# Two MLPs behind a linear attention: the second MLP's two layers mixed product by product, with its accumulators in six PSUM banks

## The chip, the cores and the metric

The kernel runs on one core of a Trainium2 chip. TensorE (PE in the tables) multiplies; each product needs its stationary operand loaded first (PEld). ScalarE (ACT) and VectorE (DVE) do the elementwise work, GpSimd (POOL) a little, and SyncE (SP) issues the DMAs. Each engine runs its own instructions in the order in which they were written. The metric is the time of one execution on the device, in microseconds (us).

## The reference

```
attn: per batch b of 4, head h of 8, over t in 0..767, with a 48x48 state:
    y_t = r_t (state + (u*k_t) outer v_t);  state = w_t * state + k_t outer v_t
x = attn as [3072 tokens, 384]
h = x @ w_in;  g = h if h > 0 else exp(h) - 1;  x = g @ w_out        # first MLP, 384 -> 2048 -> 384
h = x @ w_in2; g = h * sigmoid(h);              out = g @ w_out2     # second MLP, same sizes
```

Everything is float32. The kernel keeps that precision by writing each operand of a product as a rounded high half and a remainder, the low half, and adding three products: high by high, high by low, low by high.

## The kernel before

The program has three stretches. At first the attention of the first four units runs alone (to about 42 us); then the first MLP runs over six blocks of 512 tokens, with the attention of the next block placed between its products (to about 540 us); then the second MLP runs over the same six blocks (to the end).

The hidden width of 2048 is cut into 16 slices (`f`). One call of `slot(m, j, ..., f)` is one slice of block `j` of MLP `m`; I call it a slot. In a slot of the second MLP:

- `hidden` issues nine first-layer products, 512 columns wide, into the accumulator `ph` (line 443). There are two `ph` banks (pool `ps_h`).
- `split_g` makes the halves `gh` (ScalarE, line 465) and `gl` (VectorE, line 466) of the slice before.
- `act_begin` applies Silu to `ph` (ScalarE, line 454).
- `flush_out` takes the slice of two slots earlier (`LAG = 2`) off the list `pend` and issues its twelve second-layer products, 384 columns wide, with 128-column pieces of `gh` and `gl` as the stationary operand (`out_second`, line 482). They add to four accumulators `po`, one for each 128 tokens. After the last slice of a block, `evac_second` copies the four accumulators out, two on ScalarE and two on VectorE, in turn (`os`, lines 507 and 509), and stores them.

So the second-layer products of a block's last slice (15) are issued in the slot of slice 1 of the next block, and the slot after it is the first with the next block's second-layer products. In the first MLP a slot is alike, but the second layer has nine products 512 wide (`out_first`, line 474), and the end of a block copies three accumulators out (`x2s`, lines 491 and 493).

The second MLP's weights are prepared below the slots of the first MLP's last block and the first slots of the second MLP: `w_join` (VectorE, lines 414 and 416), `w_scale` (ScalarE, 405 and 407), `w_split` (`wh` on ScalarE, line 428, then `wl` on VectorE, line 429), one weight slice per slot.

The order on each engine is the order of the calls (`manual_schedule`); waits are added where a tile is read or a buffer reused. PSUM has eight banks: two in `ps_h`, three each in `ps_o` and `ps_a`. The second MLP's four `po` take three of `ps_o` and one of `ps_a`.

Of the kernel before, what the change touches and what calls it, by code (L numbers as in the profile page):

```python
# [7 lines left out]
F32 = mybir.dt.float32  # L8
# [10 lines left out]
LAG = 2  # L19
# [15 lines left out]
def kernel(  # L35
# [21 lines left out]
    nc = tc.nc  # L57
    B, H, S, D = r.shape
    NT, DM = out.shape
# [6 lines left out]
    KT = DM // 128  # L66
    NF = DFF // 128
# [7 lines left out]
    ps_o = ctx.enter_context(tc.tile_pool(name="ps_o", bufs=3, space=PSUM))  # L75
    ps_a = ctx.enter_context(tc.tile_pool(name="ps_a", bufs=3, space=PSUM))
# [311 lines left out]
    wh, wl = {}, {}  # L388
# [45 lines left out]
            w_load()  # L434


    def hidden(m, xt, nt, f):
        ph = ps_h.tile([128, nt], F32, tag="h", name="ph")
        n = 0
        for kt in range(KT):  # L440
            a, b = wh["i", f][:, kt * 128:(kt + 1) * 128], wl["i", f][:, kt * 128:(kt + 1) * 128]
            for lhs, rhs in ((a, "h"), (a, "l"), (b, "h")):
                nc.tensor.matmul(ph, lhs, xt[rhs][:, kt, 0:nt], start=n == 0, stop=n == 3 * KT - 1)  # L443
                n += 1
        return ph

    def act_begin(m, ph, nt):
        g = g_p.tile([128, nt], F32, tag="g", name="g")
        if m == 0:
            nc.scalar.activation(out=g, in_=ph, func=ACTF.Exp)  # L450

            nc.scalar.activation(out=g, in_=g, func=ACTF.Relu, scale=-1.0, bias=1.0)  # L452
        else:
            nc.scalar.activation(out=g, in_=ph, func=ACTF.Silu)  # L454
        return g

    def act_end(m, g, ph):
        if m == 0:
            nc.vector.scalar_tensor_tensor(  # L459
                out=g, in0=g, scalar=-1.0, in1=ph, op0=ALU.mult, op1=ALU.max)  # L460

    def split_g(m, g, nt):
        gh = g_p.tile([128, nt], F32R, tag="gh", name="gh")
        gl = g_p.tile([128, nt], F32R, tag="gl", name="gl")
        nc.scalar.activation(out=gh, in_=g, func=ACTF.Copy)  # L465
        nc.vector.tensor_tensor(out=gl, in0=g, in1=gh.bitcast(F32), op=ALU.subtract)  # L466
        return gh, gl

    def out_first(po, gs, nt, f):
        gh, gl = gs  # L470
        for ot in range(KT):
            a, b = (t["o", f][:, ot * 128:(ot + 1) * 128] for t in (wh, wl))
            for i, (lhs, rhs) in enumerate(((a, gh), (a, gl), (b, gh))):
                nc.tensor.matmul(  # L474
                    po[ot][:, 0:nt], lhs, rhs, start=f == 0 and i == 0, stop=f == NF - 1 and i == 2)

    def out_second(po, gs, nt, f):
        gh, gl = gs
        for t in range(nt // 128):
            sl = slice(t * 128, (t + 1) * 128)  # L480
            for i, (lhs, rhs) in enumerate(((gh, wh), (gh, wl), (gl, wh))):
                nc.tensor.matmul(  # L482
                    po[t][:, 0:DM], lhs[:, sl], rhs["o", f], start=f == 0 and i == 0,
                    stop=f == NF - 1 and i == 2)

    def evac_first(po, nt, tok):
        for ot in range(KT):
            pool = stage["x"] if ot == 1 and "x" in stage else o_p
            o = pool.tile([128, nt], F32, tag="o", name="x2s")
            if ot == 1:  # L490
                nc.vector.tensor_copy(o, po[ot][:, 0:nt])
            else:
                nc.scalar.activation(out=o, in_=po[ot][:, 0:nt], func=ACTF.Copy)  # L493
            nc.sync.dma_start(x2_d[:, ot, bass.ds(tok, nt)], o)
# [5 lines left out]
    def evac_second(po, nt, tok, rows=unit_rows, pool=None, final=False):  # L500
        for t in range(nt // 128):
            o = (pool or o_p).tile([128, DM], F32, tag="o", name="os")
            cut = 0 if t % 2 else DM
            if final and t == nt // 128 - 1:
                cut = DM // 2
            if cut:
                nc.scalar.activation(out=o[:, 0:cut], in_=po[t][:, 0:cut], func=ACTF.Copy)
            if cut < DM:
                nc.vector.tensor_copy(o[:, cut:], po[t][:, cut:DM])
            nc.sync.dma_start(out[bass.ds(rows(tok + t * L), L), :], o)  # L510
# [180 lines left out]
    pend, po = [], {}  # L691
    last = None

    def flush_out():
        m, j, f, nt, tok, g = pend.pop(0)
        if f == 0:
            if m == 0:
                po[m, j] = [ps_o.tile([128, nt], F32, tag="o", name="po") for _ in range(KT)]
            else:
                po[m, j] = [ps_o.tile([128, DM], F32, tag="o", name="po") for _ in range(3)]  # L700
                po[m, j].append(ps_a.tile([128, DM], F32, tag="att", name="po"))
        (out_first, out_second)[m](po[m, j], g["s"], nt, f)
        if f == NF - 1 and m == 0:
            evac_first(po[m, j], nt, tok)
        elif f == NF - 1:
            evac_second(po[m, j], nt, tok, pool=stage["o"], final=j == NB - 1)

    def slot(m, j, xt, nt, tok, f, tick=lambda part: None):
        nonlocal last
        ph = hidden(m, xt, nt, f)  # L710
        if last is not None:
            last[1]["s"] = split_g(last[0], last[1]["g"], last[2])
        g = act_begin(m, ph, nt)
        tick(0)
        act_end(m, g, ph)
        rec = {"g": g}
        last = (m, rec, nt)
        if len(pend) >= LAG:
            flush_out()
        pend.append((m, j, f, nt, tok, rec))  # L720
        tick(1)
# [10 lines left out]
    with tc.manual_schedule():  # L732
# [25 lines left out]
        for j, units in enumerate(BLOCKS):  # L758
            nt, final = units * L, j == len(BLOCKS) - 1
# [4 lines left out]
            def tick(part):  # L764
                nonlocal at
                at += 1
                done = count - 6 * len(ticks) - len(todo)
                if alone:
                    prep_rest(at, FIRST[j + 1], alone)
                wait, end = DELAY if alone else 0, END if j == 0 else 2 * NF - 2  # L770
                while done < count and done * (end - wait) < (at - wait) * count:
                    if not todo:
                        todo.extend(round_ticks(ticks.pop(0)))
                    todo.pop(0)()
                    done += 1
                if j == 0 or final and f % 4 != 3:
                    w_tick(part)

            for f in range(NF):
                slot(0, j, xts[j], nt, FIRST[j] * L, f, tick)  # L780
                if final:
                    if f == 0:
                        attn.close()
                        far_decays(0)
                        stage_open(4)
                        stage["x"] = staging.enter_context(tc.tile_pool(name="o3", bufs=1))
                        stage["o"] = staging.enter_context(tc.tile_pool(name="o2", bufs=4))
                    if f in (2, 4):
                        far_decays(f // 2)
                    if f == 0:  # L790
                        w_start(1)
                    if f == 8:
                        load_x2(0)
                    if f in (11, 12, 13):
                        split_x2(0, f - 11)
# [5 lines left out]
        for j in range(NB):  # L801
            for f in range(NF):
                if f == 8 and j + 1 < NB:
                    load_x2(j + 1)
                if f in (11, 12, 13) and j + 1 < NB:
                    split_x2(j + 1, f - 11)
                slot(1, j, x2t[j], TB, j * TB, f, w_tick)
        last[1]["s"] = split_g(last[0], last[1]["g"], last[2])
        while pend:
            flush_out()  # L810
# [65 lines left out]
    def whole_mlp(m, nt, load, evac):  # L876
        xt = x_tile(nt)
        load(xt["l"].bitcast(F32))
        split_x(xt, slice(0, nt), xt["l"].bitcast(F32), nc.vector)
        if m == 0:  # L880
            po = [ps_o.tile([128, nt], F32, tag="o", name="po") for _ in range(KT)]
        else:
            po = [ps_o.tile([128, DM], F32, tag="o", name="po") for _ in range(3)]
            po.append(ps_a.tile([128, DM], F32, tag="att", name="po"))
        for f in range(NF):
            ph = hidden(m, xt, nt, f)
            g = act_begin(m, ph, nt)
            act_end(m, g, ph)
            (out_first, out_second)[m](po, split_g(m, g, nt), nt, f)
        evac(po)  # L890
# [101 lines left out]
```

## Time and profile before

| | |
|---|---|
| median of 3 runs | 949.76 us (948.05 to 950.05) |
| profiled execution, its own time | 947.38 us |
| its span, first to last instruction | 945.6 us |
| PE busy | 918.1 us, 97% |
| ACT, DVE busy | 502.4 us (53%), 489.4 us (52%) |
| granted TensorE clock over the span | 0.981 |

The profile is of one execution; the time beside its span holds what lies around the instructions. A busy share says how much of the span an engine had an instruction running; which engine sets the end is read from the chain of work that ended last and from who waits for whom.

### The profile page before, as it was taken

How to read it: one execution, taken by the hardware profiler on the slowest of the kernel's cores; microseconds unless marked ns; L12 is line 12 of the kernel's file. 1: busy time of each engine (PE TensorE's matmuls, PEld its weight loads, DVE VectorE, ACT ScalarE, POOL GpSimd, SP SyncE). 2: the span in 40 equal slices, each digit the busy share in tenths (PEclk: the TensorE clock that was granted, in tenths of full speed). 3: DMA queues.
4: the chain of work that ended last, by engine and by line, in shares of the span. 5: the costliest groups of instructions: out<-in, count | busy, mean ns of one | idle time of the engine just before them, and what ended most of it. 6: DMA issues, size and time to landing. Idle time of an engine off the chain costs nothing.

```text
span 945.6 us, 15205 instructions
## 1 busy us (share of the span) xinstructions
PE 918.1 (97%) x6158; PEld 790.8 (84%) x6158; DVE 489.4 (52%) x726; ACT 502.4 (53%) x901; POOL 133.9 (14%) x101
## 2 busy tenths in 40 slices
PE   7779899999999999999999999999999999999996
PEld 7667688888888888888888899999999999999996
DVE  7798877776666776666378762212212212222211
ACT  6788866665655655555488963323323333333332
POOL 0000012443453334453000000000000000000000
PEclk8799999999999999999999999999999999999998
DMA  8644414222322221220245330100200200200001
GB/s 252 184 153 161 163 48 124 69 67 57 110 67 73 91 66 57 78 68 1 101 141 193 136 99 1 67 0 1 68 1 1 68 1 1 67 1 1 34 1 37
DMA packets 32222, 68.69 MB, mean 73 GB/s; under 512 B 3600, under 2 KB 13968, under 8 KB 32144
## 3 DMA queue, kind: packets, MB, share of 16 engines
q1 hardware_dynamic: 32144, 67.64, 22.5%
q8 instruction: 50, 0.82, 0.4%
q14 instruction: 28, 0.23, 0.1%
HBM read 58.19 MB, written 9.44 MB: 72 GB/s over the span
## 4 chain that ended last, share of the span: by engine, by line
PE 89%; DVE 6%; DMA 2%; ACT 2%; issue 1%; SPq 0%; DVEq 0%; ACTq 0%
PE ph L443 40%; PE po L482 21%; PE po L474 19%; PE sc L295 2%; PE y L361 2%; PE y L342 1%; DVE wst L414 1%; PE ktp L253 1%; DVE wl L429 1%; DVE wst L416 1%; DMA in_v<-in_v_tok_dram 1%; DVE am L304 1%; DVE gl L466 1%; PE upd L316 1%; DMA above_sb<-in_above_dram 1%
## 5 line engine op out<-in xcount | busy, mean ns | idle before, releaser
L466 DVE TENSOR_TENSOR gl<-g,gh 128x512 fp32r<-128x512 f32 x192 | 144.8, 754 | 313.5 <-ACT gh L465 313.3
L443 PE MATMUL ph<-xh,wh 128*128 128x512 f32 x576 | 227.6, 395 | 2.1 <-DVE g L459 2.1
L443 PE MATMUL ph<-xh,wl 128*128 128x512 f32 x576 | 227.4, 395 | 0.0
L443 PE MATMUL ph<-xl,wh 128*128 128x512 f32 x576 | 227.2, 394 | 0.0
L465 ACT ACTIVATE gh<-g 128x512 fp32r<-128x512 f32 x192 | 120.8, 629 | 153.7 <-PE po L482 109.7
L454 ACT ACTIVATE g<-ph 128x512 f32<-128x512 f32 x96 | 57.4, 598 | 137.8 <-PE ph L443 137.1
L482 PE MATMUL po<-wh,gl 128*128 128x384 f32 x384 | 129.5, 337 | 0.0
L482 PE MATMUL po<-wh,gh 128*128 128x384 f32 x384 | 129.3, 337 | 0.0
L482 PE MATMUL po<-wl,gh 128*128 128x384 f32 x384 | 128.9, 336 | 0.0
L443 PEld LDWEIGHTS ph<-xh,wl 128*128 128x128 f32 x576 | 108.7, 189 | 23.5
L443 PEld LDWEIGHTS ph<-xh,wh 128*128 128x128 f32 x576 | 109.1, 189 | 22.4 <-DVE g L459 2.5
L443 PEld LDWEIGHTS ph<-xl,wh 128*128 128x128 f32 x576 | 108.8, 189 | 19.5
L474 PE MATMUL po<-gh,wh 128*128 128x512 f32 x288 | 114.7, 398 | 0.0
L474 PE MATMUL po<-gl,wh 128*128 128x512 f32 x288 | 113.0, 392 | 0.0
L474 PE MATMUL po<-gh,wl 128*128 128x512 f32 x288 | 112.7, 391 | 0.0
L450 ACT ACTIVATE g<-ph 128x512 f32<-128x512 f32 x96 | 56.5, 589 | 52.2 <-PE ph L443 52.1
L459 DVE SCALAR_TENSOR_TENSOR g<-g,ph 128x512 f32<-128x512 f32 x96 | 65.4, 681 | 27.7 <-ACT g L452 27.1
L482 PEld LDWEIGHTS po<-wh,gh 128*128 128x128 f32 x384 | 72.2, 188 | 4.3 <-ACT x2s L493 0.2
L482 PEld LDWEIGHTS po<-wl,gh 128*128 128x128 f32 x384 | 72.1, 188 | 4.1
L482 PEld LDWEIGHTS po<-wh,gl 128*128 128x128 f32 x384 | 72.0, 188 | 0.0
L233 POOL TENSOR_TENSOR ql<-tq,qh 64x512 fp32r<-64x512 f32 (+1 forms) x30 | 42.7, 1423 | 167.1 <-ACT qh L232 166.0
L474 PEld LDWEIGHTS po<-gh,wh 128*128 128x128 f32 x288 | 54.5, 189 | 11.8 <-issue 0.8
(92 smaller groups left out, 1078.6 us busy)
## 6 DMA issues: line engine op xcount, KB each, us to landing
wst<-in_moe_w_in_dram SPq DMA_DIRECT2D x32, 384.0 KB, 3.2
wst<-in_moe_w_out_dram SPq DMA_DIRECT2D x32, 384.0 KB, 4.0
in_c<-in_rk_ch_dram SPq DMA_DIRECT2D x24, 448.0 KB, 3.8
in_w<-in_w_ch_dram SPq DMA_DIRECT2D x24, 226.2 KB, 2.7
in_v<-in_v_tok_dram SPq DMA_DIRECT2D x24, 224.0 KB, 3.1
x_d<-x2s SPq DMA_DIRECT2D x18, 256.0 KB, 2.4
xl<-x_d SPq DMA_DIRECT2D x6, 768.0 KB, 5.3
out_dram<-os SPq DMA_DIRECT2D x24, 192.0 KB, 2.0
```

Source lines behind the costliest of these rows:

```text
L233: nc.gpsimd.tensor_tensor(out=lo, in0=x, in1=hi.bitcast(F32), op=ALU.subtract)
L253: nc.tensor.transpose(p[:, j, :], st["kd"][:, j, :], ident[0:RB, 0:RB])
L295: nc.tensor.matmul(p[:, jj].rearrange("p e t -> p (e t)"), a[:, j, :], b[:, j].rearrange("p e t -> p (e t)"), start=i == 0, stop=i == len( ...
L361: nc.tensor.matmul(y[32 * base:32 * base + 32, blk // 4, :], vf[:, c:c + 32], st["a"][:, h // 2, h % 2, :], start=not ch and step == 0, st ...
L443: nc.tensor.matmul(ph, lhs, xt[rhs][:, kt, 0:nt], start=n == 0, stop=n == 3 * KT - 1)
L450: nc.scalar.activation(out=g, in_=ph, func=ACTF.Exp)
L454: nc.scalar.activation(out=g, in_=ph, func=ACTF.Silu)
L459: nc.vector.scalar_tensor_tensor(out=g, in0=g, scalar=-1.0, in1=ph, op0=ALU.mult, op1=ALU.max)
L465: nc.scalar.activation(out=gh, in_=g, func=ACTF.Copy)
L466: nc.vector.tensor_tensor(out=gl, in0=g, in1=gh.bitcast(F32), op=ALU.subtract)
L474: nc.tensor.matmul(po[ot][:, 0:nt], lhs, rhs, start=f == 0 and i == 0, stop=f == NF - 1 and i == 2)
L482: nc.tensor.matmul(po[t][:, 0:DM], lhs[:, sl], rhs["o", f], start=f == 0 and i == 0, stop=f == NF - 1 and i == 2)
```

## The change

`hidden` takes a list of further products and issues them between its own, evenly: behind the n-th of its nine, as many as n/9 of the list. `flush_out` can be handed a function, to which it gives the second layer's products one by one (`out_second_parts`) in place of issuing them itself. A slot of the second MLP, from the third on, first calls `flush_out` with such a function, so that the twelve second-layer products of the slice two slots back stand between the nine first-layer products of its own slice. The work behind it follows in program order: the copies of `evac_second` (or `evac_first`), which stood behind `split_g` and Silu, now stand ahead of them. The four `po` of a block take banks of `ps_o` and `ps_a` in turn, two of each, so that six banks rotate.

```diff
-    def hidden(m, xt, nt, f):
+    def hidden(m, xt, nt, f, others=()):
         ph = ps_h.tile([128, nt], F32, tag="h", name="ph")
-        n = 0
+        n = done = 0
...
                 nc.tensor.matmul(ph, lhs, xt[rhs][:, kt, 0:nt], start=n == 0, stop=n == 3 * KT - 1)
                 n += 1
+                while done * 3 * KT < n * len(others):
+                    others[done]()
+                    done += 1
         return ph
...
+    def out_second_parts(po, gs, nt, f):
+        gh, gl = gs
+
+        def part(t, i):
+            lhs, rhs = ((gh, wh), (gh, wl), (gl, wh))[i]
+            nc.tensor.matmul(
+                po[t][:, 0:DM], lhs[:, t * 128:(t + 1) * 128], rhs["o", f], start=f == 0 and i == 0,
+                stop=f == NF - 1 and i == 2)
+
+        return [lambda t=t, i=i: part(t, i) for t in range(nt // 128) for i in range(3)]
+
     def out_second(po, gs, nt, f):
...
+        for part in out_second_parts(po, gs, nt, f):
+            part()
...
-    def flush_out():
+    def flush_out(between=None):
         m, j, f, nt, tok, g = pend.pop(0)
...
-                po[m, j] = [ps_o.tile([128, DM], F32, tag="o", name="po") for _ in range(3)]
-                po[m, j].append(ps_a.tile([128, DM], F32, tag="att", name="po"))
-        (out_first, out_second)[m](po[m, j], g["s"], nt, f)
+                po[m, j] = [pool.tile([128, DM], F32, tag=tag, name="po")
+                            for pool, tag in ((ps_o, "o"), (ps_a, "att")) * 2]
+        if between:
+            between(out_second_parts(po[m, j], g["s"], nt, f) if m else ())
+        if m == 0 or not between:
+            (out_first, out_second)[m](po[m, j], g["s"], nt, f)
...
-        ph = hidden(m, xt, nt, f)
+        ph = None
+
+        def both_layers(others):
+            nonlocal ph
+            ph = hidden(m, xt, nt, f, others)
+
+        if m == 1 and len(pend) >= LAG:
+            flush_out(both_layers)
+        else:
+            both_layers(())
         if last is not None:
             last[1]["s"] = split_g(last[0], last[1]["g"], last[2])
```

On TensorE, at an ordinary slot of the second MLP (the slot of slice 9 of its first block; `ph` is the first layer's accumulator, `po` the second's, `wh9` and `wl9` the weight halves of slice 9). Before:

```order
L443 MATMUL ph_7295<-xh_6791,wh9_1_5528 128x512 [waits Activation_49]
L443 MATMUL ph_7295<-xl_6792,wh9_1_5528 128x512
L443 MATMUL ph_7295<-xh_6791,wl9_1_5529 128x512
L443 MATMUL ph_7295<-xh_6791,wh9_1_5528 128x512
L443 MATMUL ph_7295<-xl_6792,wh9_1_5528 128x512
L443 MATMUL ph_7295<-xh_6791,wl9_1_5529 128x512
L443 MATMUL ph_7295<-xh_6791,wh9_1_5528 128x512
L443 MATMUL ph_7295<-xl_6792,wh9_1_5528 128x512
L443 MATMUL ph_7295<-xh_6791,wl9_1_5529 128x512
L482 MATMUL po_7108<-wh7_1_5448,gh_7277 128x384 [waits Activation_49]
L482 MATMUL po_7108<-wl7_1_5449,gh_7277 128x384
L482 MATMUL po_7108<-wh7_1_5448,gl_7278 128x384 [waits DVE_49]
```

Of the change, from the same place:

```order
L444 MATMUL ph_7295<-xh_6791,wh9_1_5528 128x512 [waits Activation_49]
L486 MATMUL po_7092<-wh7_1_5448,gh_7289 128x384 [waits Activation_49]
L486 MATMUL po_7092<-wl7_1_5449,gh_7289 128x384
L444 MATMUL ph_7295<-xl_6792,wh9_1_5528 128x512
L486 MATMUL po_7092<-wh7_1_5448,gl_7290 128x384 [waits DVE_49]
L444 MATMUL ph_7295<-xh_6791,wl9_1_5529 128x512
L486 MATMUL po_7093<-wh7_1_5448,gh_7289 128x384
L444 MATMUL ph_7295<-xh_6791,wh9_1_5528 128x512
L486 MATMUL po_7093<-wl7_1_5449,gh_7289 128x384
L486 MATMUL po_7093<-wh7_1_5448,gl_7290 128x384
L444 MATMUL ph_7295<-xl_6792,wh9_1_5528 128x512
L486 MATMUL po_7094<-wh7_1_5448,gh_7289 128x384
```

The product that needs `gh` has moved from tenth to second in the slot, and the one that needs `gl` from twelfth to fifth; the widths 512 and 384 alternate, with a pair of 384 at three places.

On ScalarE, at the end of the first MLP (`x2s` copies out the first MLP's last accumulators, the `gh` in the piece are those of the second MLP's first two slices, `g` is Silu's output, `wst` and `wh` are weight preparation). Before:

```order
L428 ACTIVATE wh10_1_5591<-wst_5385 128x768 [waits DVE_49]
L465 ACTIVATE gh_5608<-g_5576 128x512 [waits PE_49,Activation_49]
L454 ACTIVATE g_5612<-ph_5598 128x512 [waits PE_49]
L405 ACTIVATE wst_5492<-wst_5492 128x768 [waits DMAHW3_49,DMAHW2_49]
L407 ACTIVATE wst_5492<-wst_5492 128x768
L493 ACTIVATE x2s_5627<-po_5081 128x512 [waits PE_49]
L493 ACTIVATE x2s_5633<-po_5083 128x512 [waits PE_49]
L428 ACTIVATE wh11_1_5636<-wst_5452 128x768 [waits DVE_49]
L465 ACTIVATE gh_5653<-g_5612 128x512 [waits Activation_49]
```

Of the change:

```order
L428 ACTIVATE wh10_1_5591<-wst_5385 128x768 [waits DVE_49]
L503 ACTIVATE x2s_5617<-po_5081 128x512 [waits PE_49]
L503 ACTIVATE x2s_5623<-po_5083 128x512 [waits PE_49]
L469 ACTIVATE gh_5626<-g_5585 128x512 [waits Activation_49]
L458 ACTIVATE g_5630<-ph_5598 128x512
L405 ACTIVATE wst_5492<-wst_5492 128x768 [waits DMAHW3_49,DMAHW2_49]
L407 ACTIVATE wst_5492<-wst_5492 128x768
L428 ACTIVATE wh11_1_5636<-wst_5452 128x768 [waits DVE_49]
L469 ACTIVATE gh_5669<-g_5630 128x512 [waits Activation_49]
```

The two copies, which wait for TensorE's last products of the first MLP, have moved ahead of the first `gh` of the second MLP.

On VectorE, where the second MLP's first block ends (`os` copies out `po` of 128 tokens, the second and the fourth of four). Before:

```order
L466 TENSOR_TENSOR gl_6061<-g_6036,gh_6060 128x512 [waits DVE_49,PE_49,Activation_49]
L466 TENSOR_TENSOR gl_6089<-g_6064,gh_6088 128x512 [waits DVE_49,PE_49,Activation_49]
L466 TENSOR_TENSOR gl_6117<-g_6092,gh_6116 128x512 [waits DVE_49,PE_49,Activation_49]
L509 COPY os_6137<-po_5664 128x384 [waits PE_49]
L509 COPY os_6143<-po_5666 128x384 [waits PE_49]
L466 TENSOR_TENSOR gl_6157<-g_6120,gh_6156 128x512 [waits DVE_49,Activation_49]
```

Of the change:

```order
L470 TENSOR_TENSOR gl_6073<-g_6048,gh_6072 128x512 [waits DVE_49,PE_49,Activation_49]
L470 TENSOR_TENSOR gl_6101<-g_6076,gh_6100 128x512 [waits DVE_49,PE_49,Activation_49]
L519 COPY os_6131<-po_5644 128x384 [waits PE_49]
L519 COPY os_6137<-po_5646 128x384 [waits PE_49]
L470 TENSOR_TENSOR gl_6141<-g_6104,gh_6140 128x512 [waits DVE_49,Activation_49]
L470 TENSOR_TENSOR gl_6173<-g_6144,gh_6172 128x512 [waits DVE_49,Activation_49]
```

`gl_6117` before and `gl_6141` of the change are the same half, that of slice 0 of the next block: it stood ahead of the two copies and now stands behind them. On ScalarE the two `os` copies and the `gh` of that slice have changed places in the same way.

## Rows read from the trace of the kernel before

**Rows 1.** The page: busy time; the chain that ended last; the Silu group.

```profile
PE 918.1 (97%) x6158; PEld 790.8 (84%) x6158; DVE 489.4 (52%) x726; ACT 502.4 (53%) x901; POOL 133.9 (14%) x101
...
PE 89%; DVE 6%; DMA 2%; ACT 2%; issue 1%; SPq 0%; DVEq 0%; ACTq 0%
...
L454 ACT ACTIVATE g<-ph 128x512 f32<-128x512 f32 x96 | 57.4, 598 | 137.8 <-PE ph L443 137.1
```

**Rows 2.** Busy time by window: PE, PEld, DVE, ACT, POOL, clock, DMA share, GB/s.

```profile
544.65:921.45 376.80, 376.80 (x1891) 341.46 (x1891) 89.72 (x129) 130.29 (x216) 0.00 (x0) 1.00 0.08 25
```

**Rows 3.** Timeline of TensorE, second MLP: start, length, line, operation.

```profile
599.08 0.39 PE L443 MATMUL ph<-xh,wh 128*128 128x512 f32 x1
599.31 0.40 PE L443 MATMUL ph<-xl,wh 128*128 128x512 f32 x1
...
603.26 0.39 PE L443 MATMUL ph<-xh,wh 128*128 128x512 f32 x1
603.50 0.40 PE L443 MATMUL ph<-xl,wh 128*128 128x512 f32 x1
...
605.35 0.33 PE L482 MATMUL po<-wh,gh 128*128 128x384 f32 x1
605.52 0.34 PE L482 MATMUL po<-wl,gh 128*128 128x384 f32 x1
...
606.41 0.33 PE L482 MATMUL po<-wh,gh 128*128 128x384 f32 x1
...
607.45 0.39 PE L443 MATMUL ph<-xh,wh 128*128 128x512 f32 x1
607.68 0.40 PE L443 MATMUL ph<-xl,wh 128*128 128x512 f32 x1
```

**Rows 4.** Timeline of TensorE: a first-MLP product, and the first 384-wide one.

```profile
501.76 0.39 PE L474 MATMUL po<-gh,wh 128*128 128x512 f32 x1
...
542.56 0.34 PE L482 MATMUL po<-wh,gh 128*128 128x384 f32 x1
```

**Rows 5.** Timelines of TensorE, ScalarE and VectorE at the first block's end.

```profile
607.28 0.33 PE L482 MATMUL po<-wh,gl 128*128 128x384 f32 x1
...
607.13 0.49 ACT L507 ACTIVATE os<-po 128x384 f32<-128x384 f32 x1 [0.57 <-PE po L482]
607.54 0.63 ACT L465 ACTIVATE gh<-g 128x512 fp32r<-128x512 f32 x1
...
607.65 0.56 DVE L509 COPY os<-po 128x384 f32<-128x384 f32 x1 [0.48 <-PE po L482]
608.20 0.69 DVE L466 TENSOR_TENSOR gl<-g,gh 128x512 fp32r<-128x512 f32 x1
```

**Rows 6.** Timelines of ScalarE and VectorE at the second MLP's first slots.

```profile
539.17 0.66 ACT L465 ACTIVATE gh<-g 128x512 fp32r<-128x512 f32 x1
541.80 1.08 ACT L493 ACTIVATE x2s<-po 128x512 f32<-128x512 f32 x2
...
544.61 0.69 DVE L466 TENSOR_TENSOR gl<-g,gh 128x512 fp32r<-128x512 f32 x1
546.20 0.96 DVE L416 SCALAR_TENSOR_TENSOR wst<-wst 128x768 int32<-128x768 int32 x1
547.19 0.92 ACT L428 ACTIVATE wh<-wst 128x768 fp32r<-128x768 f32 x1 [0.85 <-DVE wst L416]
548.15 0.96 DVE L429 TENSOR_TENSOR wl<-wst,wh 128x768 fp32r<-128x768 f32 x1 [0.99 <-ACT wh L428]
549.02 0.69 DVE L466 TENSOR_TENSOR gl<-g,gh 128x512 fp32r<-128x512 f32 x1
...
561.32 0.96 DVE L429 TENSOR_TENSOR wl<-wst,wh 128x768 fp32r<-128x768 f32 x1 [0.96 <-ACT wh L428]
```

**Rows 7.** Timeline of TensorE's weight loads: one that waited for a copy.

```profile
542.45 0.19 PEld L482 LDWEIGHTS po<-wh,gh 128*128 128x128 f32 x1 [0.15 <-ACT x2s L493]
```

More of the change, by code (lines that the diff above doesn't have):

```diff
@@ L475, in out_first @@
                     po[ot][:, 0:nt], lhs, rhs, start=f == 0 and i == 0, stop=f == NF - 1 and i == 2)
-    def out_second(po, gs, nt, f):
[L478 to L484, printed above, removed]
+    def out_second_parts(po, gs, nt, f):
[6 more added lines that the diff above has]
+        return [lambda t=t, i=i: part(t, i) for t in range(nt // 128) for i in range(3)]
+    def out_second(po, gs, nt, f):
+        for part in out_second_parts(po, gs, nt, f):
+            part()
     def evac_first(po, nt, tok):
```

## The prediction

> **What bounds the kernel now.** The page comes first: PE is busy for 97% of the span, and the chain that ended last runs through PE for 89% of it, with the other engines at 6% and less [rows 1]. So a change counts for what it does to PE's spacing or to PE's waits. The windows come next. One cut through the second MLP, from the first product of one slot to that of the slot 90 further on, holds 1891 products, 90 times 21 and one, in 376.80 us, at a granted clock of 1.00, the 2.4 GHz level [rows 2]. PE never pauses there, and a slot takes 376.80 / 90 = 4.187 us.
>
> The timeline then shows what 21 products cost. In the first MLP, where all are 512 wide, 180 products lie between 501.76 and 542.56: 40.80 / 180 = 0.2267 us each [rows 4]. In a second-MLP slot the last six 384-wide ones run from 606.41 to 607.45: 1.04 / 6 = 0.1733 us each [rows 3]. A slot with nothing else would be 9 x 0.2267 + 12 x 0.1733 = 2.040 + 2.080 = 4.120 us. So 0.067 us of a slot goes to something that neither width costs by itself. The last six are free of it; it lies in the fifteen products that follow a change from a run of 384 to a run of 512. No wait explains it, and I don't know its cause. The change touches just this, the order of widths, and besides that it moves when PE needs `gh` and `gl`.
>
> **Term A, the spacing.** Nothing is added or removed: nine and twelve products stay, in 94 of the 96 slots mixed (the first two issue the first MLP's second layer; the last two groups of `po` stand alone at the end). The trace has no alternating widths, so I bound this. If mixing lets nothing settle badly, the whole 0.067 goes: 94 x 0.067 = 6.3 us less. If PE never gets out of the disturbed state, all 21 products carry what now fifteen do: 0.067 x 21 / 15 = 0.093, which is 0.027 x 94 = 2.5 us more. The nearest rows are first products after a change of width. First 512 after 384: 599.08 to 599.31, 603.26 to 603.50, 607.45 to 607.68, or 0.23, 0.24, 0.23, mean 0.233; first 384 after 512: 605.35 to 605.52, 0.17 [rows 3]. A pair is 0.403 against a clean 0.400. Nine pairs a slot give 0.027, and 0.027 x 94 = 2.5 us stays of the 6.3: A = -3.8 us. These rows are rounded to 0.01, and they follow long runs, so I keep both ends.
>
> A rule of the chip bears on this. The fifteen disturbed products cost 0.067 us over the two settled spacings [rows 2 to 4]. The Trainium skill, "TensorE: Matmul & The Clock Gate", section "Back-to-back issue gap", gives an isolated gap from the product's own width and the clock, with no term for its neighbours; by that, order would change nothing, A would be 0, and the sum, by the waits below alone, about 956 us.
>
> **Term B, the ends of five blocks.** At the end of a block the `os` copies now stand ahead of the next block's first `gh` and `gl`, while PE wants these earlier. Take T as the start of the slot that finishes the block and T' = T + 4.12 as the next. The third accumulator's last product is sixteenth in its slot, behind seven 512 and eight 384: T + 7 x 0.2267 + 8 x 0.1733 = T + 2.97. It lasts 0.33, and a copy starts 0.04 after a product's end (607.28 + 0.33 = 607.61, the copy at 607.65); so ScalarE's second `os` starts at T + 3.34. `gh` starts 0.41 behind an `os` (607.13, 607.54) and takes 0.63 [rows 5]: it ends at T + 4.38, or T' + 0.26. A load starts about 0.04 later, and the product comes 0.11 behind a late load (542.45 and 542.56 [rows 4, 7]): T' + 0.41, where its place is T' + 0.23.
>
> VectorE is worse. The fourth accumulator's last product ends the slot, starting at T' - 0.17 and ending at T' + 0.16; its copy starts at T' + 0.20; `gl` starts 0.55 behind (607.65, 608.20) and takes 0.69 [rows 5], to T' + 1.44. With load and product, T' + 1.59; its place, fifth, is 0.227 + 2 x 0.173 + 0.227 = T' + 0.80. PE loses 0.8 us, the 0.2 on `gh` included. In the kernel before, the nine `ph` products (2.1 us) and a slot more covered this. The end of blocks 0 to 4: B = 5 x 0.8 = +4.0 us. All of PE stands behind the waiting load.
>
> **Term C, the entry.** The first mixed slot would start where the last nine `ph` before 542.56 do: 542.56 - 9 x 0.2267 = 540.52 [rows 4]. The first MLP's last product starts 0.23 earlier and lasts 0.39: 540.68. Both `x2s` now stand ahead of the first `gh`, which before ran at 539.17. The second `x2s` starts at 540.72 and takes half of 1.08; `gh` (0.66) [rows 6] ends at about 541.91, the product needing it starts at 542.06, and its place was 540.75: 1.3 us late. `gl` follows, 541.95 to 542.64, its product at 542.79 against 542.06 + 0.57 = 542.63: 0.16 more.
>
> The slots behind it carry weight preparation. On VectorE and ScalarE a chain leads from one `gl` through the weight work to the next: 544.61 to 549.02, or 4.41 us a slot, with `wh` waiting for line 416 and `wl` for `wh`, until the last `wl` at 561.32 [rows 6], so that five more `gl` end such a chain. Before, PE reached the product that needs `gl` 1.6 us later in its slot and had that as cover. Now the next `gl` ends at 541.95 + 4.41 + 0.69 = 547.05 and its product starts at 547.20; its place, with the delay so far, is 540.52 + 4.12 + 1.46 + 0.80 = 546.90: 0.3 late. Each of the four after it gains 4.41 - 4.12 = 0.29 on PE. C = 1.3 + 0.16 + 0.3 + 4 x 0.29 = +2.9 us; with slots of 4.187 the chain gains only 0.22 each and C is 2.6.
>
> **What costs nothing.** In an ordinary slot Silu now waits for a `ph` that ends with the slot; Silu 0.60 [rows 1], `gh` 0.63 and `gl` 0.69 [rows 5] end about 2 us into the next slot, and PE wants them a slot later, so about 2 us of cover remain. At the program's end only twelve products (2.08 us) cover the same chain, just enough; if not, some tenths once. The six banks keep the next block's first two accumulators off the banks being copied; the other two are free by the middle of the slot.
>
> **Sum.** A - 3.8, B + 4.0, C + 2.9: +3.1 us. The profiled execution took 947.38, span 945.6; it lies 2.4 below the median of 949.76, so I put the difference on the median: about 953 us, +0.33%. About 0.2% (1.9 us) is what a measurement of this kernel can tell from no change.
>
> **Rivals.**
> 1. Spacing settles fully (A = -6.3): -6.3 + 6.9 = +0.6, 950.4 us. For it: the first 384 after 512 shows 0.17, nothing extra. Against: one change disturbs fifteen products now, so a state is carried from product to product, and a mixed slot changes width eighteen times.
> 2. Order does not matter to the spacing, 4.187 stays: 4.0 + 2.6 = +6.6, 956.4 us. For it: a cost paid per 384-wide product would be paid in any order. Against: the settled six.
> 3. PE never settles: 2.5 + 6.6 = +9.1, 958.9 us. For it: changes will come every product or two, long before fifteen products are over. Against: the first products behind a change cost next to nothing more [rows 3].
> 4. Faster: mixing also shortens the gap that each settled product has beyond its columns (128 columns make 0.2267 - 0.1733 = 0.0534 us, so 512 make 0.2133, and 0.0133 us is left at either width), since neighbours now write different banks. A quarter of it, 0.0033 x 21 x 94 = 6.6, with all of the 6.3: -12.9 + 6.9 = -6.0, 943.8 us. It decides once the two save 8.8 us together, 0.094 a slot. Against: in the first MLP `po` changes bank every third product and the mean is 0.2267 all the same.
>
> **Chances.** Forecast (spacing between) 0.28, rival 1 0.25, rival 2 0.22, rival 3 0.16, rival 4 0.09. Rival 1 falls within 0.2% but for a little, and a fifth of the forecast's case does: faster 0.10, same 0.30, slower 0.60. The range runs from just under rival 1 to rival 3: 949.5 to 959; it leaves out rival 4 and some of the outer cases.
>
> **What would show it.** A right: PE's slots in the undisturbed middle of a block at 4.12 to 4.19 us (clean 4.120, rival 3 4.21). B right: five times, behind the `os` copies, PE's load waits first for `gh` 0.2, then for `gl` 0.6 us. C right: one wait of 1.3 us near 541 behind `x2s`, then about 0.3 in each of five slots, each ended by `gl`. The forecast falls if PE's list of waits stays empty in the second MLP, or if the slot there is under 4.09 us or over 4.22.

## The result, and the profile after

The changed kernel takes 959.5 us (median of 4 runs, 958.47 to 961.78) against 949.9 us beside it (948.05 to 951.64): ratio 1.0109, 95% interval 1.0091 to 1.0127. It is slower by about 9.6 us, just beyond the upper end of the forecast's range.

From the page after, the same lines as in [rows 1]:

```profile
PE 929.5 (97%) x6158; PEld 794.1 (83%) x6158; DVE 487.9 (51%) x726; ACT 501.5 (52%) x901; POOL 133.6 (14%) x101
...
PE 90%; DVE 5%; ACT 2%; issue 1%; DMA 1%; SPq 0%; DVEq 0%; ACTq 0%
...
L458 ACT ACTIVATE g<-ph 128x512 f32<-128x512 f32 x96 | 57.4, 598 | 249.1 <-PE ph L444 249.1
```

PE still bounds the kernel, with the same 6158 products, and is busy 11.4 us longer, but at the same share of 97%: the busy share doesn't show a larger distance between products. Silu now waits 249.1 us for `ph` (137.1 before), as foreseen, and neither PE nor its loads wait for Silu.

Busy time by window, as in [rows 2]: the first six mixed slots, ten undisturbed ones in block 0, fifteen in block 1.

```profile
544.15:571.71 27.56, 26.58 (x128) 22.33 (x127) 18.72 (x23) 18.84 (x27) 0.00 (x0) 1.00 0.36 115
571.71:614.11 42.40, 42.40 (x212) 38.17 (x211) 8.59 (x13) 14.19 (x25) 0.00 (x0) 1.00 0.03 10
619.02:682.62 63.60, 63.60 (x317) 57.30 (x316) 12.05 (x18) 20.34 (x35) 0.00 (x0) 1.00 0.03 10
```

The cuts lie at first products of slots. An undisturbed slot takes 42.40 / 10 = 63.60 / 15 = 4.240 us, at a clock of 1.00: 0.053 more than the 4.187 before, 0.120 more than a clean 4.120. The six entry slots take 27.56 instead of 25.44: 2.12 us of stalls.

TensorE's timeline in the middle of block 1, one third of a slot:

```profile
640.22 0.40 PE L444 MATMUL ph<-xh,wh 128*128 128x512 f32 x1
640.46 0.34 PE L486 MATMUL po<-wh,gh 128*128 128x384 f32 x1
640.63 0.34 PE L486 MATMUL po<-wl,gh 128*128 128x384 f32 x1
640.81 0.39 PE L444 MATMUL ph<-xl,wh 128*128 128x512 f32 x1
641.04 0.34 PE L486 MATMUL po<-wh,gl 128*128 128x384 f32 x1
641.22 0.40 PE L444 MATMUL ph<-xh,wl 128*128 128x512 f32 x1
641.46 0.34 PE L486 MATMUL po<-wh,gh 128*128 128x384 f32 x1
641.63 0.40 PE L444 MATMUL ph<-xh,wh 128*128 128x512 f32 x1
```

From 640.22 to 641.63 there are three 512s and four 384s in 1.41 us; settled they would take 3 x 0.2267 + 4 x 0.1733 = 1.373. No row has a wait: the 0.04 is spacing.

The waits of TensorE's weight loads in the second MLP (us in total, times, longest), where before PE waited for nothing and its loads once, for 0.15 us [rows 7]:

```profile
PEld po L486 <- DVE gl L470: 5.0, 11, 0.7
...
PEld po L486 <- ACT gh L469: 2.6, 6, 1.4
```

Eleven waits for `gl` and six for `gh`. The entry, from the timelines of ScalarE, VectorE, TensorE and its loads:

```profile
544.35 0.60 ACT L503 ACTIVATE x2s<-po 128x512 f32<-128x512 f32 x1 [0.76 <-PE po L478]
544.85 0.62 ACT L469 ACTIVATE gh<-g 128x512 fp32r<-128x512 f32 x1
...
545.50 0.69 DVE L470 TENSOR_TENSOR gl<-g,gh 128x512 fp32r<-128x512 f32 x1 [0.97 <-ACT gh L469]
549.90 0.68 DVE L470 TENSOR_TENSOR gl<-g,gh 128x512 fp32r<-128x512 f32 x1
...
545.52 0.19 PEld L486 LDWEIGHTS po<-wh,gh 128*128 128x128 f32 x1 [1.40 <-ACT gh L469]
```

`gh` starts behind the second `x2s` and the load waits 1.40 us for it. The next `gl` comes 549.90 - 545.50 = 4.40 us later, at the pace of the weight preparation, so each of the five slots behind takes about 4.39. The first mixed slot takes the rest of the 27.56, 5.61 us, or 1.37 more than 4.240. The end of block 0, the slot from 614.11:

```profile
613.30 0.49 ACT L517 ACTIVATE os<-po 128x384 f32<-128x384 f32 x1 [1.75 <-PE po L486]
613.69 0.62 ACT L469 ACTIVATE gh<-g 128x512 fp32r<-128x512 f32 x1
...
614.30 0.56 DVE L519 COPY os<-po 128x384 f32<-128x384 f32 x1 [1.68 <-PE po L486]
614.78 1.41 DVE L470 TENSOR_TENSOR gl<-g,gh 128x512 fp32r<-128x512 f32 x2
...
614.37 0.19 PEld L486 LDWEIGHTS po<-wh,gh 128*128 128x128 f32 x1 [0.25 <-ACT gh L469]
615.51 0.19 PEld L486 LDWEIGHTS po<-wh,gl 128*128 128x128 f32 x1 [0.68 <-DVE gl L470]
```

First `gh`, then `gl`, each behind an `os`. That slot takes 619.02 - 614.11 = 4.91 us and the other four 4.93 each: 0.67 + 4 x 0.69 = 3.4 us of stalls.

Sum: spacing 94 x 0.053 = 5.0, entry 2.1, block ends 3.4: 10.5 us. From the first mixed slot to the end of the span lie 960.0 - 544.15 = 415.85 us, before (from the place that the prediction names) 945.6 - 540.52 = 405.08: 10.8 more. The rest of what lies between the two spans is ahead of the first mixed slot (544.15 against 540.52 us), where the programs are alike. Between the medians it is 9.6; the profiled execution, at 961.78, is the longest of the four.

### The profile page after: what moved, and what is told of

Same layout as the page of the kernel before. It is cut to its first block, busy times and chain, and to the rows that moved or that the text cites. A ratio compares the mean times of both kernels' runs of the same rounds, so it can differ in the third digit from the quotient of the medians.

```text
span 960.0 us, 15110 instructions
## 1 busy us (share of the span) xinstructions
PE 929.5 (97%) x6158; PEld 794.1 (83%) x6158; DVE 487.9 (51%) x726; ACT 501.5 (52%) x901; POOL 133.6 (14%) x101
## 4 chain that ended last, share of the span: by engine, by line
PE 90%; DVE 5%; ACT 2%; issue 1%; DMA 1%; SPq 0%; DVEq 0%; ACTq 0%
PE ph L444 40%; PE po L486 21%; PE po L478 20%; PE sc L295 2%; PE y L361 2%; PE y L342 1%; PE ktp L253 1%; PE sc L287 1%; DVE gl L470 1%; DVE wst L416 1%; DVE wst L414 1%; DMA in_c<-in_rk_ch_dram 1%; PE upd L316 1%; DVE wl L429 1%; DVE am L304 0%
## 5 line engine op out<-in xcount | busy, mean ns | idle before, releaser
L444 PE MATMUL ph<-xh,wh 128*128 128x512 f32 x576 | 230.1, 400 | 1.1 <-DVE g L463 1.1
L458 ACT ACTIVATE g<-ph 128x512 f32<-128x512 f32 x96 | 57.4, 598 | 249.1 <-PE ph L444 249.1
L444 PEld LDWEIGHTS ph<-xl,wh 128*128 128x128 f32 x576 | 108.9, 189 | 10.5
```

## The experiments

**The stalls.** `e1_halves_first` returns the copies from `flush_out` and issues them behind Silu:

```diff
-        if f == NF - 1 and m == 0:
-            evac_first(po[m, j], nt, tok)
-        elif f == NF - 1:
-            evac_second(po[m, j], nt, tok, pool=stage["o"], final=j == NB - 1)
+        def evac():
+            if f == NF - 1 and m == 0:
+                evac_first(po[m, j], nt, tok)
+            elif f == NF - 1:
+                evac_second(po[m, j], nt, tok, pool=stage["o"], final=j == NB - 1)
+
+        if between:
+            return evac
+        evac()
...
+            evac = flush_out(both_layers)
...
         g = act_begin(m, ph, nt)
+        if evac:
+            evac()
         tick(0)
```

> The changed kernel, but the copies of finished accumulators (x2s, os) are issued behind gh, gl and Silu of the slot. If PE's waits come from the program order of these copies: the first mixed slot's 1.36 us and the five block ends' 0.67 to 0.69 us go, the five slots with weight preparation lose most of their 0.15, so 5 us or so of 5.56 are won, about 954 us; the undisturbed slot stays 4.240 us. If the waits come from the chains themselves (Silu to gh to gl too long for the slot), they stay, and so does 959.

Measured: 955.8 us, ratio to before 1.0073 (1.0054 to 1.0092). Its loads' waits in the second MLP:

```profile
PEld po L486 <- DVE gl L470: 1.5, 5, 0.4
PEld po L486 <- ACT x2s L503: 0.3, 1, 0.3
...
601.93:669.77 67.84, 67.84 (x338) 61.15 (x337) 13.99 (x21) 21.55 (x37) 0.00 (x0) 1.00 0.07 24
```

The waits at the block ends and the long one at the entry are gone: they came from the order of the copies. The part about the five slots with weight preparation fell: four still take 4.40 and one 4.51, so they lose nothing of their 0.15, and the entry costs about 1.1 us in all. The undisturbed slot stays 4.240 (sixteen in the last line, 67.84 / 16), and 5.0 + 1.1 makes 6.1 of the 6.4 us by which this kernel is slower than before.

**Banks, or the mixing itself.** `e2_banks_only` is the kernel before with the six banks alone:

```diff
-                po[m, j] = [ps_o.tile([128, DM], F32, tag="o", name="po") for _ in range(3)]
-                po[m, j].append(ps_a.tile([128, DM], F32, tag="att", name="po"))
+                po[m, j] = [pool.tile([128, DM], F32, tag=tag, name="po")
+                            for pool, tag in ((ps_o, "o"), (ps_a, "att")) * 2]
```

> The kernel before with the changed kernel's six banks in turn, nothing mixed. Width theory (a change between 512-wide and 384-wide products costs time, the banks none): slot 4.187 us, time as before. Bank theory (the spacing follows from which banks the products write): slot 4.24 us, 94 times 0.053 = 5.0 us more, about 955 us.

Measured: 949.21 us, ratio 0.9997 (0.9986 to 1.0009). The window over 90 slots, the same 376.80 us as in [rows 2]:

```profile
549.16:925.96 376.80, 376.80 (x1891) 341.43 (x1891) 87.23 (x126) 128.21 (x213) 0.00 (x0) 1.00 0.06 22
```

The banks cost nothing. `e4_first_mixed` mixes the first MLP's last block in place of the second MLP, so that all products there are 512 wide:

```diff
-        if m == 1 and len(pend) >= LAG:
-            flush_out(both_layers)
...
+        if m == 0 and j == len(BLOCKS) - 1 and len(pend) >= LAG:
+            evac = flush_out(both_layers)
```

> The second MLP not mixed (as before, but with the six banks), the first MLP's last block mixed: its products are all 512 wide, 18 in a slot, and the two layers alternate one by one. Width theory: mixing products of one width costs nothing, 18 x 0.2267 = 4.080 us in undisturbed slots. Mixing theory (two accumulators and two sources in turn cost, whatever the widths): nine changes at 0.0133, 4.20 us.

Its single run took 955.2 us; some of its slots wait for `gh` and `gl`. Where nothing waits, TensorE's timeline shows:

```profile
525.06 0.39 PE L444 MATMUL ph<-xl,wh 128*128 128x512 f32 x1
525.28 0.39 PE L479 MATMUL po<-gl,wh 128*128 128x512 f32 x1
...
529.14 0.39 PE L444 MATMUL ph<-xl,wh 128*128 128x512 f32 x1
```

The rows left out go on alternating: 18 products in 529.14 - 525.06 = 4.08 us, settled. `e6_wide` asks the same in the second MLP, where `wh["w", f]` and `wl["w", f]` are the last 512 columns of the tile that holds both layers' weights:

```diff
-                po[t][:, 0:DM], lhs[:, t * 128:(t + 1) * 128], rhs["o", f], start=f == 0 and i == 0,
+                po[t], lhs[:, t * 128:(t + 1) * 128], rhs["w" if po[t].shape[-1] == 512 else "o", f], start=f == 0 and i == 0,
```

> As e1_halves_first, mixed as in the changed kernel, but the second layer's products take 512 columns of the same weight tiles instead of 384 (128 columns more, which nobody reads). If the extra spacing is the change of width, all products settle: 21 x 0.2267 = 4.760 us a slot. If it is the mixing itself in this stage (its banks, its sources): 4.760 + 0.120 = 4.880.

Measured (one run, 1004.34 us, twelve products a slot being 128 columns wider):

```profile
566.74:614.34 47.60, 47.60 (x211) 39.41 (x210) 8.72 (x13) 13.53 (x24) 0.00 (x0) 1.00 0.00 1
```

Ten slots, 4.760 each: mixing as such is free. With the operands where they lie here, the extra needs products of two widths.

**How the order of widths sets it.** `e3_runs_of_three`:

```diff
-                while done * 3 * KT < n * len(others):
+                while n % 3 == 0 and done * 3 * KT < n * len(others):
```

> As e1_halves_first, but three products of the first layer and four of the second alternate instead of one and one or two: three changes of width and back in a slot instead of nine. If each change and back costs 0.0133 us, as in the mixed slots: 4.120 + 3 x 0.0133 = 4.160 us a slot, 94 x 0.08 = 7.5 us under e1_halves_first, about 946.5. If a change disturbs the products behind it for a while (in the kernel before the first three 512s and four 384s behind a change hold 0.033 of the 0.067 us): 4.120 + 3 x 0.033 = 4.22 us, 2 us under e1_halves_first.

Measured: 954.31 us, ratio 1.0057 (1.0036 to 1.0078), and sixteen slots of block 1 in 67.85 us, 4.240 each:

```profile
601.51:669.36 67.85, 67.85 (x338) 61.01 (x338) 14.00 (x21) 21.56 (x38) 0.00 (x0) 1.00 0.08 24
```

Both figures missed: three changes a slot cost as much as nine. `e5_patterns` takes its runs from a table, by block:

```diff
+    PLANS = ([(9, 12)], [(5, 6), (4, 6)], [(6, 8), (3, 4)], [(8, 1), (1, 11)], [(7, 2), (2, 10)], [(1, 1), (8, 11)])
```

> As e1_halves_first, with another order of the nine 512s (h) and twelve 384s (p) in the slots of each of the six blocks: 9h 12p; 5h 6p 4h 6p; 6h 8p 3h 4p; 8h 1p 1h 11p; 7h 2p 2h 10p; 1h 1p 8h 11p. Runs-of-512 theory (each of the first five 512s of a run pays one step of 0.0133 us, later ones none, as the runs of 1, 3 and 9 suggest with 1, 3 and 5 steps): 5, 9, 8, 6, 7, 6 steps over 4.120, or slots of 4.187, 4.240, 4.227, 4.200, 4.213, 4.200 us. Shorter-run theory (the shorter of the two runs counts, up to five): 5, 9, 8, 2, 4, 6 steps, 4.187, 4.240, 4.227, 4.147, 4.173, 4.200. Ceiling theory (any slot with more than one change and back pays 0.120): 4.240 in all but the first.

Measured (one run, 951.45 us), ten slots of each block in turn:

```profile
573.92:615.78 41.86, 41.86 (x211) 37.94 (x211) 10.12 (x15) 14.50 (x25) 0.00 (x0) 1.00 0.07 21
619.97:661.84 41.87, 41.87 (x212) 37.97 (x212) 8.82 (x13) 13.63 (x23) 0.00 (x0) 1.00 0.00 1
682.78:724.71 41.93, 41.93 (x211) 37.86 (x211) 8.12 (x12) 13.11 (x24) 0.00 (x0) 1.00 0.06 19
749.80:791.47 41.67, 41.67 (x212) 37.75 (x211) 8.86 (x13) 13.86 (x23) 0.00 (x0) 1.00 0.05 18
812.33:854.13 41.80, 41.80 (x212) 37.87 (x211) 8.57 (x13) 13.41 (x23) 0.00 (x0) 1.00 0.12 38
887.65:929.65 42.00, 42.00 (x212) 38.01 (x211) 6.93 (x10) 12.29 (x20) 0.00 (x0) 1.00 0.00 1
```

4.186, 4.187, 4.193, 4.167, 4.180, 4.200: all three theories fell, and no count of changes gives these numbers. Long runs do follow a rule: in `e7_pairs` and `e8_fours` two and four slots' `ph` run behind each other, then as many slots' `po`:

```diff
-        if len(pend) >= LAG:
+        while len(pend) >= LAG and (m == 0 or f % 2 == 1 or pend[0][0] == 0 and f == 1):
             flush_out()
```

> The kernel before, not mixed; in the second MLP two slots' first layers run behind each other, then two slots' second layers: one change of width and back for 18 and 24 products. If a change and back between long runs costs five steps (0.067 us) whatever the length: 4.120 + 0.033 = 4.153 us a slot, 96 x 0.033 = 3.2 us faster than before, about 946.3. If each slot pays its 0.067 whatever the order, or long runs pay more: as before.

> As e7_pairs, with four slots' first layers and then four slots' second layers: 36 and 48 products between changes. Five steps for a change and back: 4.120 + 0.067 / 4 = 4.137 us a slot, 96 x 0.050 = 4.8 us faster than before, about 944.7. If the spacing has nothing to do with the number of changes: as before.

Measured: pairs 946.17 us, ratio 0.9962 (0.9950 to 0.9974); fours 948.19 us, 0.9981 (0.9967 to 0.9994). Undisturbed slots take 4.153 and 4.137 us in their traces, as expected: 0.067 for each change and back, shared by two or four slots. Twenty slots of the pairs, 83.06 / 20:

```profile
601.16:684.22 83.06, 83.06 (x421) 75.62 (x421) 17.82 (x27) 27.59 (x47) 0.00 (x0) 1.00 0.12 39
```

Both kernels also keep `gh` and `gl` in a pool of their own; the last block of `e17_g_address` (below) has such a pool too and takes the 4.187 of before, which speaks against the pool as the cause. The fours lose most of their gain at the entry, where TensorE waits 2.4 us for Silu behind the weight preparation. So `e11_fours_late` takes pairs there and fours later:

```diff
+        while len(pend) >= LAG and (m == 0 or f % 4 == 3 or j == 0 and f < 8 and f % 2):
```

> As e8_fours from the middle of the second MLP's first block on, and as e7_pairs ahead of it, where e8_fours made the third and fourth first layer wait for Silu behind the weight preparation (2.4 us on PE). Slots of 4.137 us from there on and no wait at the entry: 96 slots save about 0.033 x 8 + 0.050 x 88 = 4.7 us against before, about 945.5 us, and 1.4 less than e7_pairs. If the wait comes back at another place: no less than e7_pairs.

Measured: 944.99 us, ratio 0.9955 (0.9941 to 0.9968), faster than both kernels. Ten groups of four slots, 165.47 / 40 = 4.137:

```profile
610.42:775.89 165.47, 165.47 (x842) 151.02 (x841) 35.13 (x53) 54.95 (x94) 0.00 (x0) 1.00 0.09 29
```

**Other widths.** In `e9_widths` and `e10_widths_long` each block has its own width:

```diff
+WIDTH = (512, 416, 448, 480, 496, 384)
```

> As e6_wide (mixed, gh, gl and Silu ahead of the copies), with another width of the second layer's products in each of the six blocks: 512, 416, 448, 480, 496, 384 columns, so another difference to the first layer's 512. With a settled product at its columns plus 0.0133 us (estimate from 0.2267 at 512 and 0.1733 at 384) the slots without extra are 4.760, 4.280, 4.440, 4.600, 4.680, 4.120. If any change of width costs one step of 0.0133: 0.120 more in all but the first block (4.400, 4.560, 4.720, 4.800, 4.240). If the cost goes with the difference of the widths: 0.120 x 96/128 = 0.090, 0.060, 0.030, 0.015, 0.120 more (4.370, 4.500, 4.630, 4.695, 4.240).

> As e9_widths, but not mixed: nine 512s, then twelve of the block's width. Fixed cost of a change and back (0.067 us between long runs): 4.760, then 4.347, 4.507, 4.667, 4.747, 4.187. Cost by the difference: 4.760, then 4.330, 4.473, 4.617, 4.688, 4.187.

Measured, one run each: mixed 4.760, 4.400, 4.540, 4.720, 4.770, 4.240; long 4.760, 4.320, 4.487, 4.654, 4.773, 4.187. The cost by the difference fell in both. One step for any change gives four of the six mixed slots but not 448 and 496, and the fixed cost misses the four middle ones of the long runs by 0.013 to 0.027 us. Nor does the base that they share hold. Ten slots with 496s in the long run, and two of its products:

```profile
850.98:898.71 47.73, 47.73 (x212) 39.48 (x210) 9.00 (x13) 13.86 (x23) 0.00 (x0) 1.00 0.00 0
...
862.57 0.39 PE L488 MATMUL po<-wh,gh 128*128 128x496 f32 x1
...
864.16 0.39 PE L488 MATMUL po<-wl,gh 128*128 128x496 f32 x1
```

Seven products take 1.59 us, 0.227 each, as much as 512s. These runs also changed the column at which a read begins: 256, 352, 320, 288, 272 and 384. Counted within 64 columns, which the next runs show to matter, 352, 288 and 272 are other places than 384, so for 416, 480 and 496 width and place can't be told apart. At 448 (column 320) only the width differs: over a base of 4.440 (an estimate, by columns plus 0.0133 us a product) the extra is 0.100 mixed and 0.047 long, between the 0.120 and 0.067 of 384 and the nothing of 512. The place was then tried by itself.

**Where the columns lie.** `e12_address` keeps 384 columns and lets them begin elsewhere (outside the last block it multiplies by partly other columns than the second layer's own); `e13_address_mixed` and `e14_address_long` do so with other places, most of them inside a step of 64 columns:

```diff
-                po[t][:, 0:DM], lhs[:, t * 128:(t + 1) * 128], rhs["o", f], start=f == 0 and i == 0,
+                po[t], lhs[:, t * 128:(t + 1) * 128], rhs["w", f][:, c:c + DM], start=f == 0 and i == 0,
...
+            between(out_second_parts(po[m, j], g["s"], nt, f, (0, 32, 64, 128, 256, 384)[j]) if m else ())
```

> As e1_halves_first, mixed, second layer's products 384 wide in all blocks, but their 384 weight columns begin at another place of the weight tile in each block: column 0, 32, 64, 128, 256, 384 of its 768 (only in the last block is that the second layer's own weights; the other blocks multiply by partly wrong columns, so the output is not the reference's there). If the extra follows from the widths: 4.240 us a slot in every block. If it follows from where the products read, which the width changed too in e6_wide and e9_widths: other slots in some blocks, 4.120 where the start suits.

> As e12_address, mixed, with the 384 columns beginning at column 8, 16, 32, 48, 96, 224 of the weight tile (8, 16, 32, 48, 32, 32 modulo 64; the output is not the reference's). If the place within 64 columns (256 bytes) sets it: 4.180 us at 32, 96 and 224 alike, something else between 4.120 and 4.240 at 8, 16 and 48. If column 32 was a peculiarity of that block (its banks, its time): 4.240 in all, or 4.180 in the second block alone.

> As e13_address_mixed, but not mixed (nine 512s, then twelve 384s), beginning at column 8, 16, 32, 48, 96, 384. If the read address acts on the change between long runs too: another slot than 4.187 us at 8 to 96, and one value for 32 and 96. If the 0.067 us there has nothing to do with addresses: 4.187 in all six blocks.

One run each. `e12_address` had 4.180 in the block at column 32 and 4.240 in the others, so the theory of the widths alone fell. Ten of its slots at 32 and ten at 64:

```profile
620.09:661.88 41.79, 41.79 (x211) 37.81 (x211) 8.73 (x13) 13.51 (x23) 0.00 (x0) 1.00 0.00 0
687.08:729.48 42.40, 42.40 (x211) 38.21 (x211) 8.72 (x13) 13.52 (x23) 0.00 (x0) 1.00 0.00 1
```

`e13_address_mixed`: 4.200 at 8, 4.180 at 16, 4.180 at 32, 96 and 224 alike, 4.171 at 48. `e14_address_long`, ten slots at 16, at 32 and at 384:

```profile
617.84:659.17 41.33, 41.33 (x211) 37.70 (x211) 9.00 (x13) 13.85 (x23) 0.00 (x0) 1.00 0.00 1
684.02:725.62 41.60, 41.60 (x211) 37.95 (x211) 8.99 (x13) 13.86 (x23) 0.00 (x0) 1.00 0.00 1
...
883.73:925.60 41.87, 41.87 (x212) 37.95 (x212) 6.92 (x10) 12.29 (x20) 0.00 (x0) 1.00 0.00 1
```

4.133, 4.160 and 4.187 (4.160 at 8, 48 and 96 too): the place within 64 columns (256 bytes) acts on both orders. `e15_shift` and `e16_shift_fours` move all weight tiles by 64 bytes and keep every product:

```diff
+    ctx.enter_context(tc.tile_pool(name="ahead", bufs=1)).tile([128, 16], F32, name="ahead")
     wpool = ctx.enter_context(tc.tile_pool(name="wts", bufs=1))
+    ctx.enter_context(tc.tile_pool(name="behind", bufs=1)).tile([128, 48], F32, name="behind")
```

> The kernel before, its order unchanged; only all weight tiles lie 16 columns (64 bytes) further on. If the read address sets the spacing: the second MLP's slot goes to 4.133 us as in e14_address_long at column 16, 96 x 0.053 = 5.1 us faster than before, about 944.4. If e14_address_long was faster for another reason (other values, the tile's first columns): 4.187 and as before.

> As e11_fours_late with the same shift. If the changes of width and the address act on one and the same cost: a change and back costs 0.013 instead of 0.067 us, a slot 4.120 + 0.013 / 4 = 4.123, about 0.064 x 96 = 6 us faster than before, 943.5, and 1.2 faster than e11_fours_late. If the address does nothing: as e11_fours_late, 4.137 and 945.

Measured: both 957.3 us, ratios 1.0087 (1.0072 to 1.0102) and 1.0081 (1.0068 to 1.0094). Both expectations fell. The slot is 4.180 in both, and in `e15_shift` the first MLP's 512s, one width only, no longer settle:

```profile
503.54 0.40 PE L445 MATMUL ph<-xh,wh 128*128 128x512 f32 x1
...
504.94 0.40 PE L445 MATMUL ph<-xh,wh 128*128 128x512 f32 x1
```

Six products take 1.40 us, 0.233 each against 0.227, at a granted clock of 1.00. In the second MLP the same is seen, and a change of width costs nothing more there. From `e16_shift_fours`, the first products of a run of thirty-six 512s, of the forty-eight 384s behind it and of the next run:

```profile
662.25 0.39 PE L445 MATMUL ph<-xh,wh 128*128 128x512 f32 x1
...
670.64 0.34 PE L485 MATMUL po<-wh,gh 128*128 128x384 f32 x1
...
678.97 0.39 PE L445 MATMUL ph<-xh,wh 128*128 128x512 f32 x1
```

That is 8.39 / 36 = 0.233 and 8.33 / 48 = 0.1735 us a product, and 16.72 / 4 = 9 x 0.2333 + 12 x 0.1733 is the 4.180, so longer runs gain nothing in this layout. The shift moved the loaded weights of both first layers and of the first MLP's second layer, too. `e17_g_address` moves only `gh` and `gl`, the loaded weights of the second layer:

```diff
+    COLUMN = (8, 16, 32, 48, 24, 0)
...
+        gh = pool.tile([128, w], F32R, tag="gh", name="gh")[:, c:c + nt]
+        gl = pool.tile([128, w], F32R, tag="gl", name="gl")[:, c:c + nt]
```

> The kernel before, its order unchanged; in the second MLP gh and gl (the weights loaded for the second layer's products) begin 8, 16, 32, 48, 24, 0 columns further on in their tiles, by block. If what counts is the place of the loaded weights relative to the columns read: slots other than 4.187 us in the first five blocks, one of them (48 is the reverse of the shift by 16) near 4.133, and 4.187 in the last. If only the place of the columns read counts: 4.187 in all six.

Measured (one run, 947.14 us): 4.173, 4.173, 4.200, 4.160, 4.166, 4.187. Ten slots each at 48 and at 0:

```profile
751.10:792.70 41.60, 41.60 (x211) 37.73 (x211) 9.01 (x13) 13.86 (x23) 0.00 (x0) 1.00 0.00 1
...
884.38:926.25 41.87, 41.87 (x212) 37.94 (x212) 6.92 (x10) 12.29 (x20) 0.00 (x0) 1.00 0.00 1
```

So the place of the loaded weights counts as well, though 48 doesn't give the 4.133 of its counterpart.

## Why the prediction was wrong

**What bounds the kernel** held: PE does, and spacing plus waits make up the difference.

**Term B** (+4.0) held in place, order and nearly in size: five times, `gh` then `gl` behind `os`, 3.4 us. The estimate for `gl` was 0.8 a time, the trace has 0.67 to 0.69; `e1_halves_first` shows the cause.

**Term C** (+2.9) held in its two parts: 1.37 us in the first mixed slot behind `x2s` (1.46 predicted, for `gh` and `gl` together), then the weight preparation's pace, 4.40 (4.41 predicted). With slots of 4.24 instead of 4.12 the chain gains only 0.15 a slot on PE, so that C is 2.1.

**Term A is the step that failed**: -3.8 predicted, +5.0 measured, above its upper bound (+2.5). It let mixing give back most of the 0.067 us that a slot of long runs loses; in its place the mixed slot loses 0.120, and the prediction's own mark, a slot over 4.22, was passed. Together B and C were 6.9 predicted and 5.5 measured, so A's error of 8.8 us is what put the time out of range, and the smaller waits hid 1.4 of it. Two readings failed in it. The "nearest rows", first products behind a change between long runs, gave 0.003 us a pair; in the mixed slot a change and back costs 0.120 / 9 = 0.013. And the upper bound took the mean of the long runs' fifteen disturbed products (0.067 / 15 = 0.0045 us each) as the worst there is; 0.120 / 21 = 0.0057 is more. A bound drawn from the one pattern that a trace holds is not a bound for another.

**Rival 3** (PE never settles) had the direction, and its 958.9 is nearest to the result, but partly by luck: its spacing was too small (+2.5 for +5.0), its waits too large (6.6 for 5.5). No run shows that a state carried from product to product is what costs the time.

**Rival 2** (order does not matter) fell: 4.137 to 4.240 us by order alone. Beside it stood the rule of the Trainium skill, "TensorE: Matmul & The Clock Gate", section "Back-to-back issue gap", whose isolated gap has no term for neighbours; these runs disagree, by 0.103 us a slot. **Rival 4**'s idea that neighbours in different banks shorten the gap fell too: equal widths keep 0.2267 when mixed (`e4_first_mixed`, `e6_wide`).

**What stays open**: by what mechanism the widths and the places of the operands set the spacing. Shown is that the extra goes away with equal widths in the old layout, that it falls there with fewer changes between long runs, and that it moves with the place of both the columns read and the weights loaded, so far that after the shift of `e15_shift` the 512s cost more by themselves and the changes nothing. Not shown is a rule that gives 4.240, 4.187 and 4.167 from an order.

## What to carry to other kernels

Where PE bounds and never waits, an order of products is worth its spacing: cut one window over many slots, compare it with the settled widths, and keep products of one width in long runs (here 0.067 us for each change and back; fewer of them made the kernel 0.45% faster). That holds for one place of the operands: with the weight tiles 64 bytes further on, runs four times as long gained nothing (957.3 us both ways). A product placed earlier takes the cover from what it reads: list who issues ahead of the producer on its engine, and put copies that nobody is waiting for behind it. Where a trace holds only one pattern, price another one wide on both sides, or measure it in blocks of one run, as the tables by block did here.

## What was not expected of the hardware

The spacing of products depends on where their operands lie within 256 bytes: 4.133 to 4.187 us for the same slot of long runs. A shift of the weight tiles by 64 bytes took the first MLP's equal products from 0.227 to 0.233 us. And 496 columns took as long as 512 in long runs (0.227 us), but they began at another place within the 256 bytes, so this may be the place and not the width.
